# Third batch's softmax and second weights' split placed behind the second batch's last first-step evictions, on one Trainium2 core

## The chip, the cores and the metric

One of the cores of a Trainium2 chip runs the whole program. The metric is the device time of one execution in microseconds (us). Five engines work side by side, each through its own queue of instructions and in that queue's order: PE (matrix products), DVE (VectorE), ACT (ScalarE), POOL (GpSimd) and SP, which here only starts DMAs. An instruction at the head of a queue waits until what it needs is there, and all behind it wait with it.

## The reference

For each of 8 batches, x is 4224 rows of 192 columns. Each row has 8 heads of 24 columns, and each head has 7 weights.

```python
w = weight_gen - np.max(weight_gen, axis=-1, keepdims=True)
w = np.exp(w)
w = w / (np.sum(w, axis=-1, keepdims=True) + 1e-09)       # softmax over the 7 taps
...
out = np.einsum('bshk,bskhg->bshg', w, x_unf)              # causal convolution, 7 rows, weights by row and head
...
X = np.fft.fft(x, axis=1)                                  # x is now the convolution's result
X = np.fft.fft(X, axis=2)
mixed = np.real(X).astype(np.float32)
u = x + mixed
un = (u - mu) / np.sqrt(var + 1e-06)                       # over the 192 columns
ch = np.maximum(un @ w_ch1, 0.0) @ w_ch2                   # 192 -> 768 -> 192
return (u + ch).astype(np.float32)
```

The two weights of the last line come as 64-bit floats.

## The kernel before

A batch's 4224 rows lie as 33 slots of 128 partitions. Five stages follow each other in a batch, and stages of neighbouring batches overlap. In names below, b is the batch, c a chunk and g a group.

*Softmax* (`softmax_taps`). DVE takes the maximum over the taps (L279) and subtracts it (L280), ACT takes Exp in place (L282), DVE sums (L284), adds 1e-9 (L285) and takes the reciprocal (L286) into a PSUM tile `wp`. From batch 2 on this is done for all 33 slots at once (`parts` of one piece). The generator yields between the steps, and `tap_step(b, n)` drives it to its n-th yield: the first follows the load of the weights, the second the Exp, the third the reciprocal.

*Convolution* (`conv`). Chunks 0 to 7 hold four slots each, chunk 8 (`NC`) a single one. Per chunk DVE makes the normalized weights `wp` (L372 and L375), then seven products (L441): the first straight into `u`, the others into `pr`, from a ring of five buffers. POOL adds each `pr` to `u` (L450). `DVE_ADDS` names the chunks of which DVE makes the first adds: in batch 1's chunks 2 to 7 the first two. POOL then folds mirrored slots into `sm` (L464, L466), PE takes the first step of the Fourier transform into `pg` (L471), ACT copies parts of it into `gt` and `up` (L476, L478), DVE adds and subtracts (L480, L482) into `gt`, and `gt` goes to DRAM as `g_d` (L485, L486), two chunks at a time.

*Transform* (`transform`). `g` is read back from `g_d` in another layout (L507), PE takes the second step into `pp` (L517), and ACT copies it into `pq` (L521 to L531). All of `g_d` must be there first, chunk 8 too.

*Mix and norm* (`mix`, `norm`). PE takes the transform over the columns into `eo` (L546), ACT copies half of it to `ot` (L551), DVE adds to `u` (L552 to L561). ACT takes the row statistics (L586, L590, L592), POOL a product (`rs`, L599), ACT normalizes into `un` (L601) and rounds to 16 bits into `hl` (L609), POOL writes the rest of the rounding into `hl` (L610, L612), and a transposing DMA makes `ht` (L618).

*MLP* (`mlp`). Group n is four slots, n = 9b + g. PE makes the first layer in six pieces `ph` of five terms (L643), ACT the relu `hh` (L653, or L649 in the first groups), DVE the rest of its rounding (L654). In the same stretch PE makes the second layer `po` of group n - 1 (L666), DVE adds it to `u` (L671), and `u` goes out (L675). The first seven groups (`F32_GROUPS`) use the second weights in 32 bits (`w2f`); later ones use two 16-bit parts, `w2h` and `w2l`. `split_w2` makes these: three maxima on DVE (L179), a trip through PE to have the largest of all partitions (L186, L189), a scale, then per third an ACT product into `w2h` (L220) and a DVE product less that into `w2l` (L221), and a factor `isc`.

*What sets the order.* Each stage is a stream of pieces with a start and an end, in units of MLP groups, and `run` takes the stream that is furthest behind. Then a planner simulates the queues and sets the order in which instructions really stand in them. `tc.issue_after(ins)` holds what is issued under it in that plan until after `ins`; `queue(ins, ...)` and `behind(ins, gen)` are built on it. The streams around the change:

```python
add(SPLIT + 1.0, SPLIT + 1.5, late_split())
...
pp_at, mix_at, step = (NG - HELD + 0.6, NG - HELD, 0.6) if b == 1 else (PP_AT, 3.0, MIX_STEP)
```

`late_split` is issued behind group 4's `ph` and behind batch 1's last product. The transform of batch 1 begins at 9 - 2.6 = 6.4, and from 7.0 on `held_mlp` holds group 7 until batch 1's last `pp` is issued. Batch b's convolution is issued behind the last product of batch b - 1 (`next_conv`).

Of the kernel before, what the change touches and what calls it, by code (L numbers as in the profile page):

```python
# [31 lines left out]
EARLY = 7.4  # L32
HELD = 7.0
SPLIT = 4
CONV_LEAD = 0.4
# [3 lines left out]
POOL_TAPS = {(0, 0): (5, 6), (0, 1): (5, 6), (0, 3): (6,), (1, 0): range(7), (1, 1): range(7)}  # L39
DVE_ADDS = {(1, c): 2 for c in range(2, NC)}  # L40
F32_GROUPS = 7
# [51 lines left out]
def tile_dynconv_fnet_mlp(  # L93
# [159 lines left out]
    def prep_w2(i):  # L253
        words_to_f32(loaded[1][i], w2_part(i)[0], f"w2_{i}", ("po", 2))

    def split_w2(_):
        s2 = weight_scale([w2_part(i)[0].bitcast(I32) for i in range(NH // 2)], 32, "w2")
        for i in range(NH // 2):
            split_f32(*w2_part(i), s2)
        nc.vector.tensor_tensor(out=isc, in0=scales[0][:, 1:2], in1=s2[:, 1:2], op=ALU.mult)  # L260
# [3 lines left out]
    def softmax_taps(b, parts):  # L264
# [5 lines left out]
        for lo, hi in parts:  # L270
# [3 lines left out]
            elif b == 0 and hi < N2:  # L274
# [6 lines left out]
                                    in1=m[:, sl].unsqueeze(2).broadcast_to([P, n, K]), op=ALU.subtract)  # L281
            nc.scalar.activation(w_sb[:, sl], w_sb[:, sl], AF.Exp)  # L282
            yield None
# [4 lines left out]

    taps = {}

    def tap_step(b, n):
# [15 lines left out]
    def conv(b):  # L307
# [22 lines left out]
        def need_taps(c):  # L330
            nonlocal w_sb, ws
            while not rows_w.issuperset(rows_of(c)):
                i = next(part_iter)
                rows_w.update(range(*parts[i]))
                tap_step(b, 3 * i + 3)
                w_sb, ws = taps[b]["tiles"]
# [14 lines left out]
        for grp in groups:  # L351
# [101 lines left out]
            while tails and not (b == 1 and grp[0] == 0):  # L453
# [23 lines left out]
                up = sb.tile([P, 2, D - DH], F32, tag="up", name=f"up_{b}_{c}", bufs=2)  # L477
                nc.scalar.copy(up[:, 0:J], pg[:, 0:J, DH:D])  # L478
                fwd, rev = pg[:, 0:J, 1:DH - 1], up[:, 0:J, ::-1]
# [53 lines left out]
    state, us, hls = {}, {}, {}  # L533
    last_tile, last_pg, last_product, last_fold, last_gt, last_g2, last_pp = {}, {}, {}, {}, {}, {}, {}
    pending = {}
# [207 lines left out]
    def late_split():  # L743
        yield 0.0
        with tc.issue_after(last_ph[SPLIT].ins):
            queue(last_product[1].ins, (split_w2, None))
        yield 1.0
# [20 lines left out]
    add(0.93, 0.95, late_warm(1))  # L768
    add(SPLIT + 1.0, SPLIT + 1.5, late_split())
    for b in range(B):  # L770
        t0 = NG * b
        pp_at, mix_at, step = (NG - HELD + 0.6, NG - HELD, 0.6) if b == 1 else (PP_AT, 3.0, MIX_STEP)
        if b > 0:
# [46 lines left out]
```

## Time and profile before

| | us |
|---|---|
| median of 3 runs | 1138.15 |
| lowest, highest | 1135.78, 1138.86 |
| span of the profiled execution | 1136.8 |
| PE busy in it | 1082.2 |
| DVE busy | 968.2 |
| POOL busy | 866.7 |
| ACT busy | 814.5 |

The span is from the first to the last instruction of one execution, which a hardware profiler recorded; all rows of the trace come from it, and its times count from the span's start. The profile gives no other time of that execution, so its span stands for its own time; it lies within the range of the three runs. A row of the timeline has the start, the length, the engine, the line, the operation, output and inputs, the shape, how many such instructions in a row were put together (x3), and in brackets how long the engine was idle just before and what it waited for. Lengths include a start-up that overlaps the instruction before, so from start to start is often less than a length. Matrix products in 32 bits count double in the x. A row of the windows has the length of the stretch, the busy time of PE, PE's weight loads, DVE, ACT and POOL, then the granted clock of PE as a share of full speed, the share of the DMA engines and GB/s.

The single slot of batch 1 is added up in POOL's row at 207.41, the last `gt` of batch 1 is written at 215.29, the Exp of batch 2 runs at 206.68, and PE takes batch 1's first `pp` at 223.50.

### The profile page before, as it was taken

How to read it: one execution, taken by the hardware profiler on the slowest of the kernel's cores; microseconds unless marked ns; L12 is line 12 of the kernel's file. 1: busy time of each engine (PE TensorE's matmuls, PEld its weight loads, DVE VectorE, ACT ScalarE, POOL GpSimd, SP SyncE). 2: the span in 40 equal slices, each digit the busy share in tenths (PEclk: the TensorE clock that was granted, in tenths of full speed). 3: DMA queues.
4: the chain of work that ended last, by engine and by line, in shares of the span. 5: the costliest groups of instructions: out<-in, count | busy, mean ns of one | idle time of the engine just before them, and what ended most of it. 6: DMA issues, size and time to landing. Idle time of an engine off the chain costs nothing.

```text
span 1136.8 us, 23769 instructions
## 1 busy us (share of the span) xinstructions
PE 1082.2 (95%) x8476; PEld 819.3 (72%) x8476; DVE 968.2 (85%) x1797; ACT 814.5 (72%) x2556; POOL 866.7 (76%) x747
## 2 busy tenths in 40 slices
PE   5986999999999999899999999999999999999998
PEld 3454677787777767677767877777768877787777
DVE  7988999879989999899988999999989996356443
ACT  4666785468975798568974799568965898589822
POOL 5979588699979999599969999699959999012200
PEclk9996999999999999999999999999999999999999
DMA  8353244614473248414562348414661234413221
GB/s 304 129 150 106 56 110 123 175 51 128 111 200 92 65 119 219 122 55 119 149 165 81 94 107 218 121 44 119 170 140 50 71 74 98 115 43 74 70 47 46
DMA packets 156504, 128.74 MB, mean 113 GB/s; under 512 B 108571, under 2 KB 133088, under 8 KB 156384
## 3 DMA queue, kind: packets, MB, share of 16 engines
q1 hardware_dynamic: 156384, 127.21, 42.2%
q8 instruction: 67, 1.10, 0.4%
q14 instruction: 53, 0.43, 0.1%
HBM read 61.46 MB, written 39.37 MB: 89 GB/s over the span
## 4 chain that ended last, share of the span: by engine, by line
PE 52%; DVE 16%; ACT 11%; issue 8%; POOL 7%; DMA 6%; SPq 1%; DVEq 0%; POOLq 0%; ACTq 0%
PE ph L643 22%; PE po L666 19%; DVE pr L441 6%; POOL u L450 6%; PE pp L517 4%; PE eo L546 3%; DMA g<-g_d 2%; ACT junk L590 2%; ACT junk L586 2%; PE pg L471 2%; PE pa L446 2%; ACT hh L653 2%; ACT un L601 2%; DVE hh L654 2%; DMA g_d<-gt 1%
## 5 line engine op out<-in xcount | busy, mean ns | idle before, releaser
L450 POOL TENSOR_TENSOR u<-u,pr 128x768 f32<-128x768 f32 (+1 forms) x390 | 644.5, 1675 | 71.0 <-DVE pr L441 49.6
L666 PEld LDWEIGHTS <-hh 128*128 128x128 f16 x4248 | 364.0, 98 | 74.1 <-DVE hh L654 2.2
L666 PE MATMUL po<-w2h,hh 128*128 128x192 f16 x2832 | 413.9, 246 | 1.2 <-DVE hh L654 1.0
L643 PE MATMUL ph<-ht,w1h 128*128 128x512 f16 (+1 forms) x1296 | 397.0, 363 | 5.4 <-DMA ht<-hl 2.5
L441 DVE TENSOR_TENSOR pr<-x_sb,wp 128x768 f32<-128x768 f32 (+1 forms) x415 | 354.5, 877 | 13.7 <-POOL u L450 9.9
L666 PE MATMUL po<-w2l,hh 128*128 128x192 f16 x1416 | 345.2, 246 | 0.0
L654 DVE SCALAR_TENSOR_TENSOR hh<-ph,hh 128x512 f16<-128x512 f32 (+1 forms) x390 | 246.4, 637 | 108.0 <-ACT hh L653 107.4
L653 ACT ACTIVATE hh<-ph 128x512 f16<-128x512 f32 (+1 forms) x390 | 213.3, 550 | 140.8 <-PE ph L643 114.6
L643 PE MATMUL ph<-ht,w1l 128*128 128x512 f16 (+1 forms) x864 | 311.2, 363 | 0.0
L643 PEld LDWEIGHTS <-w1h 128*128 128x128 f16 x1296 | 126.1, 99 | 93.2 <-issue 2.3
L601 ACT ACTIVATE un<-u,rs 128x192 f32<-128x192 f32 x264 | 123.7, 536 | 16.7 <-POOL hl L612 5.5
L643 PEld LDWEIGHTS <-w1l 128*128 128x128 f16 x864 | 85.4, 99 | 52.9 <-issue 5.3
L590 ACT ACTIVATE junk<-u,rs 128x192 f16<-128x192 f32 x252 | 114.2, 454 | 3.6
L610 POOL TENSOR_TENSOR hl<-un,hl 128x512 f16<-128x512 f32 (+1 forms) x69 | 75.2, 1090 | 51.9 <-issue 26.5
L586 ACT ACTIVATE junk<-u 128x192 f16<-128x192 f32 x252 | 90.8, 360 | 21.5 <-DVE u L556 17.9
L521 ACT COPY pq<-pp 97x204 f32<-97x204 f32 (+1 forms) x96 | 46.9, 489 | 57.4 <-PE pp L517 57.0
L546 PE MATMUL eo<-cs_sb,pq 97*128 97x97 f32 x544 | 84.2, 277 | 2.7 <-DVE u L556 2.7
L546 PEld LDWEIGHTS eo<-cs_sb,pq 97*128 97x128 f32 x544 | 78.1, 195 | 10.2 <-issue 4.7
L671 DVE SCALAR_TENSOR_TENSOR u<-po,isc,u 128x384 f32<-128x384 f32 (+1 forms) x122 | 72.8, 597 | 9.1 <-PE po L666 9.0
L464 POOL TENSOR_TENSOR sm<-u 128x382 f32<-128x382 f32 x64 | 65.3, 1021 | 5.8 <-DMA g_d<-gt 2.8
L599 POOL TENSOR_TENSOR rs<-rs 128x4 f32<-128x4 f32 (+1 forms) x63 | 12.8, 206 | 70.7 <-DVE rs L593 70.6
L666 PE MATMUL po<-w2f,hh 128*128 128x192 f32 x336 | 62.6, 328 | 0.0
(110 smaller groups left out, 1319.5 us busy)
## 6 DMA issues: line engine op xcount, KB each, us to landing
out_dram<-u SPq DMA_DIRECT2D x64, 384.0 KB
x_sb<-in_x_dram SPq DMA_DIRECT2D x48, 384.0 KB
g<-g_d SPq DMA_DIRECT2D x40, 336.0 KB
x_sb<-in_x_dram SPq DMA_DIRECT2D x8, 864.0 KB
g_d<-gt SPq DMA_DIRECT2D x32, 195.0 KB
g_d<-gt SPq DMA_DIRECT2D x32, 189.0 KB
w<-in_weight_gen_dram SPq DMA_DIRECT2D x6, 924.0 KB
x_sb<-in_x_dram SPq DMA_DIRECT2D x8, 672.0 KB
```

Source lines behind the costliest of these rows:

```text
L441: last_product[b] = nc.vector.tensor_tensor(out=dst, in0=rows, in1=wk, op=ALU.mult)
L450: adder.tensor_tensor(out=u, in0=u, in1=pr, op=ALU.add)
L546: nc.tensor.matmul(eo[:, e, j, :], lhsT=pq[0:DH, e, r, r:r + P], rhs=cs_sb[:, e, :], start=True, stop=True)
L586: nc.scalar.activation(junk, uv[:, t, :], AF.Identity, accum_out=st[:, t, 0:1])
L590: nc.scalar.activation(junk, uv[:, t, :], AF.Square, bias=rs[:, 2, t:t + 1], accum_out=st[:, t, 1:2])
L601: nc.scalar.activation(halves[t // 2][:, t % 2, :], uv[:, t, :], AF.Identity, bias=rs[:, 1, t:t + 1], scale=rs[:, 0, t:t + 1])
L610: lo_eng.tensor_tensor(out=hl[:, t0:t1, 2 * P:3 * P], in0=src[:, 0:t1 - t0, 0:P], in1=hl[:, t0:t1, 0:P], op=ALU.subtract)
L643: last_ph[n] = nc.tensor.matmul(ph[:, 0:T], lhsT=wt[:, cs_], rhs=ht[:, 0:T, blk], start=(i == 0), stop=(i == len(terms) - 1))
L653: nc.scalar.activation(a[:, 0:T], ph[:, 0:T], AF.Relu)
L654: nc.vector.scalar_tensor_tensor(out=l[:, 0:T], in0=ph[:, 0:T], scalar=0.0, in1=a[:, 0:T], op0=ALU.max, op1=ALU.subtract)
L666: nc.tensor.matmul(po[t // 2][:, t % 2, :], lhsT=hx[:, t], rhs=wx[:, c2, :], start=(c2 == 0 and i == 0), stop=(c2 == NH - 1 and i == len(t ...
L671: nc.vector.scalar_tensor_tensor(out=lt, in0=po[t // 2][:, 0:t % 2 + 1], scalar=scales[0][:, 1:2] if f32 else isc, in1=lt, op0=ALU.mult, o ...
```

## The change

- The softmax of batch 2 (the third): Exp is issued behind batch 1's last `up` copy, which is that of chunk 8, and sum, 1e-9 and reciprocal behind batch 1's last `gt`. Maximum and subtraction are issued as before. `tap_step` is called in two steps for that in every batch.
- `split_w2` is divided: `scale_w2` takes the scale (maxima, the trip through PE), behind batch 1's last product as before; the products into `w2h` and `w2l` and `isc` are issued behind batch 1's last `gt`. The stream `late_split` moves from 5.0 to 5.5 to 6.4 to 6.5.
- `DVE_ADDS` gets `(1, NC): KW`: the six adds of batch 1's single slot (128x192) are on DVE and not on POOL.
- `PP_1` names the 2.6 of batch 1's transform, whose value is as before.

```diff
-DVE_ADDS = {(1, c): 2 for c in range(2, NC)}
+PP_1 = 2.6
+DVE_ADDS = {**{(1, c): 2 for c in range(2, NC)}, (1, NC): KW}
...
+    def scale_w2(_):
+        scales.append(weight_scale([w2_part(i)[0].bitcast(I32) for i in range(NH // 2)], 32, "w2"))
+
     def split_w2(_):
-        s2 = weight_scale([w2_part(i)[0].bitcast(I32) for i in range(NH // 2)], 32, "w2")
+        s2 = scales[1]
         for i in range(NH // 2):
             split_f32(*w2_part(i), s2)
...
-            nc.scalar.activation(w_sb[:, sl], w_sb[:, sl], AF.Exp)
+            with after(last_up[1].ins if b == 2 else None):
+                nc.scalar.activation(w_sb[:, sl], w_sb[:, sl], AF.Exp)
...
+    def after(ins):
+        return tc.issue_after(ins) if ins is not None else nullcontext()
...
-                tap_step(b, 3 * i + 3)
+                tap_step(b, 3 * i + 2)
+                with after(last_gt[1].ins if b == 2 else None):
+                    tap_step(b, 3 * i + 3)
...
-                nc.scalar.copy(up[:, 0:J], pg[:, 0:J, DH:D])
+                last_up[b] = nc.scalar.copy(up[:, 0:J], pg[:, 0:J, DH:D])
...
         with tc.issue_after(last_ph[SPLIT].ins):
-            queue(last_product[1].ins, (split_w2, None))
+            queue(last_product[1].ins, (scale_w2, None))
+            queue(last_gt[1].ins, (split_w2, None))
...
-    add(SPLIT + 1.0, SPLIT + 1.5, late_split())
+    add(NG - PP_1, NG - PP_1 + 0.1, late_split())
...
-        pp_at, mix_at, step = (NG - HELD + 0.6, NG - HELD, 0.6) if b == 1 else (PP_AT, 3.0, MIX_STEP)
+        pp_at, mix_at, step = (PP_1, NG - HELD, 0.6) if b == 1 else (PP_AT, 3.0, MIX_STEP)
```

Lines of the changed kernel have higher numbers: by 1 up to the weights' helpers, by 4 or 5 in `softmax_taps`, by 10 from there on.

The planner makes more of it than the diff tells, so here is what stands in three queues. A name such as `gt_1_8_2093` is the tile, batch, chunk and a running number.

ACT at the end of batch 1's convolution, before:

```order
L478 COPY up_1_6_1945<-pg_1_6_1940 128x190
L282 ACT_TABLE_LOAD
L282 ACTIVATE w_2_2110<-w_2_2110 128x1848
L220 ACTIVATE w2h_85<-w2f_87,sc_w2_1855 128x384 x3
L649 ACTIVATE hh_0_5_3_1962<-ph_0_5_3_1950 128x512
L649 ACTIVATE hh_0_5_4_1984<-ph_0_5_4_1975 128x512
L649 ACTIVATE hh_0_5_5_2002<-ph_0_5_5_1993 128x512
L476 COPY gt_1_6_1943<-pg_1_7_2043 128x4
L478 COPY up_1_7_2047<-pg_1_7_2043 128x190
L476 COPY gt_1_8_2093<-pg_1_8_2091 128x2
L478 COPY up_1_8_2095<-pg_1_8_2091 128x95
L649 ACTIVATE hh_0_6_0_2035<-ph_0_6_0_2015 128x512
```

And in the changed kernel:

```order
L659 ACTIVATE hh_0_6_0_2010<-ph_0_6_0_1990 128x512
L486 COPY gt_1_6_1918<-pg_1_7_2018 128x4
L488 COPY up_1_7_2022<-pg_1_7_2018 128x190
L659 ACTIVATE hh_0_6_1_2035<-ph_0_6_1_2029 128x512
L486 COPY gt_1_8_2068<-pg_1_8_2066 128x2
L488 COPY up_1_8_2070<-pg_1_8_2066 128x95
L287 ACT_TABLE_LOAD
L287 ACTIVATE w_2_2110<-w_2_2110 128x1848
L659 ACTIVATE hh_0_6_2_2078<-ph_0_6_2_2059 128x512
L221 ACTIVATE w2h_85<-w2f_87,sc_w2_2095 128x384 x3
```

Exp and the split have moved from ahead of the copies of `pg` to behind them, and between those of chunk 7 and chunk 8 there is now a relu of group 6. On PE `pg_1_8` stood directly behind `pg_1_7`; now five `po` of group 5 and eight `ph` of group 6 stand between them, the trip of the scale through PE follows behind, and the first `pp` has as much of group 6 ahead of it as before.

DVE at the same place, before:

```order
L284 TENSOR_REDUCE wp_2_2109<-w_2_2110 128x264
L221 SCALAR_TENSOR_TENSOR w2l_86<-w2f_87,sc_w2_1855,w2h_85 128x384 x3
L285 TENSOR_SCALAR wp_2_2109<-wp_2_2109 128x264
L671 SCALAR_TENSOR_TENSOR u_0_4_337<-po_0_4_1_1837,sc_w1_889,u_0_4_337 128x384
L286 RECIPROCAL wp_2_2109<-wp_2_2109 128x264
L480 TENSOR_TENSOR gt_1_6_1943<-pg_1_7_2043,up_1_7_2047 128x2x95
L482 TENSOR_TENSOR gt_1_6_1943<-pg_1_7_2043,up_1_7_2047 128x2x95
L480 TENSOR_TENSOR gt_1_8_2093<-pg_1_8_2091,up_1_8_2095 128x95
L482 TENSOR_TENSOR gt_1_8_2093<-pg_1_8_2091,up_1_8_2095 128x95
L372 TENSOR_TENSOR wp_2_2109<-w_2_2110,wp_2_2109 128x224
L441 TENSOR_TENSOR u_2_0_2121<-x_sb_66,wp_2_2109 128x768
L441 TENSOR_TENSOR pr_2_0_1_2124<-x_sb_66,wp_2_2109 128x768
```

And now (between the rows on scales, of one column each, nothing else is left out than a `po` eviction):

```order
L492 TENSOR_TENSOR gt_1_8_2068<-pg_1_8_2066,up_1_8_2070 128x95
...
L289 TENSOR_REDUCE wp_2_2109<-w_2_2110 128x264
L191 TENSOR_SCALAR m2_w2_2088<-me_w2_2092 128x1
L290 TENSOR_SCALAR wp_2_2109<-wp_2_2109 128x264
...
L291 RECIPROCAL wp_2_2109<-wp_2_2109 128x264
L264 TENSOR_TENSOR isc_88<-sc_w1_889,sc_w2_2095 128x1
L222 SCALAR_TENSOR_TENSOR w2l_86<-w2f_87,sc_w2_2095,w2h_85 128x384 x3
L382 TENSOR_TENSOR wp_2_2109<-w_2_2110,wp_2_2109 128x224
L681 SCALAR_TENSOR_TENSOR u_0_5_466<-po_0_5_1_1989,sc_w1_889,u_0_5_466 128x384
L451 TENSOR_TENSOR u_2_0_2121<-x_sb_66,wp_2_2109 128x768
L451 TENSOR_TENSOR pr_2_0_1_2124<-x_sb_66,wp_2_2109 128x768
```

The sum, the reciprocal and the split stood ahead of the last `gt`; all of them now stand behind it, and ahead of batch 2's first products.

DVE at the end of batch 2's convolution, before:

```order
L286 RECIPROCAL wp_3_3710<-wp_3_3710 128x264
L654 SCALAR_TENSOR_TENSOR hh_1_5_1_3731<-ph_1_5_1_3702,hh_1_5_1_3731 128x512
L480 TENSOR_TENSOR gt_2_8_3619<-pg_2_8_3617,up_2_8_3621 128x95
L482 TENSOR_TENSOR gt_2_8_3619<-pg_2_8_3617,up_2_8_3621 128x95
L372 TENSOR_TENSOR wp_3_3710<-w_3_3711,wp_3_3710 128x224
L441 TENSOR_TENSOR u_3_0_3722<-x_sb_66,wp_3_3710 128x768
```

And now:

```order
L492 TENSOR_TENSOR gt_2_8_3619<-pg_2_8_3617,up_2_8_3621 128x95
L664 SCALAR_TENSOR_TENSOR hh_1_6_1_4002<-ph_1_6_1_3996,hh_1_6_1_4002 128x512
L290 TENSOR_SCALAR wp_3_3710<-wp_3_3710 128x264
L664 SCALAR_TENSOR_TENSOR hh_1_6_2_4041<-ph_1_6_2_4032,hh_1_6_2_4041 128x512
L681 SCALAR_TENSOR_TENSOR u_1_5_1737<-po_1_5_0_3944,isc_88,u_1_5_1737 128x384
L291 RECIPROCAL wp_3_3710<-wp_3_3710 128x264
L664 SCALAR_TENSOR_TENSOR hh_1_6_3_4072<-ph_1_6_3_4057,hh_1_6_3_4072 128x512
L382 TENSOR_TENSOR wp_3_3710<-w_3_3711,wp_3_3710 128x224
L451 TENSOR_TENSOR u_3_0_3722<-x_sb_66,wp_3_3710 128x768
```

Batch 2's last `gt` now stands some way further on in the MLP (group 15, whose tiles are `hh_1_6`, is at work there, and before it was group 14), and the reciprocal of batch 3 stands behind it. In POOL's queue the rounding rests `hl` of batch 1 stand six or seven adds of batch 2 earlier than before, and that of batch 2's first group two adds of batch 3 earlier. On PE the sum of the work is the same, and so is the work ahead of group 18's first `ph`; batch 2's `pg`, `pp` and `eo` stand further back among it.

More of the change, by code (lines that the diff above doesn't have):

```diff
@@ L1 @@
-from contextlib import ExitStack
+from contextlib import ExitStack, nullcontext
 import numpy as np
@@ L533, in tile_dynconv_fnet_mlp @@
     state, us, hls = {}, {}, {}
-    last_tile, last_pg, last_product, last_fold, last_gt, last_g2, last_pp = {}, {}, {}, {}, {}, {}, {}
+    last_tile, last_pg, last_product, last_fold, last_gt, last_up, last_g2, last_pp = {}, {}, {}, {}, {}, {}, {}, {}
     pending = {}
```

## The prediction

> **What bounds the kernel now.** I read the page first (which engine is full), then the time by windows (where the full engine is not), then the waits and the chain of waits there, and at last the timeline of each engine at those places.
>
> ```profile
> PE 1082.2 (95%) x8476; PEld 819.3 (72%) x8476; DVE 968.2 (85%) x1797; ACT 814.5 (72%) x2556; POOL 866.7 (76%) x747
> ...
> 217.78:334.00 116.22, 111.61 (x868) 86.99 (x867) 103.11 (x186) 90.49 (x287) 113.14 (x95) 0.99 0.46 120
> 220.00:240.00 20.00, 16.50 (x119) 13.92 (x117) 13.73 (x18) 10.99 (x30) 19.84 (x13) 0.91 0.44 113
> 223.50:227.60 4.10, 4.09 (x22) 4.05 (x23) 3.45 (x5) 2.32 (x7) 4.10 (x3) 0.58 0.44 88
> 380.00:400.00 20.00, 17.84 (x180) 15.24 (x179) 19.68 (x43) 17.89 (x68) 19.91 (x18) 0.94 0.39 99
> 400.00:420.00 20.00, 20.00 (x145) 13.84 (x144) 17.75 (x32) 19.36 (x72) 18.90 (x17) 0.97 0.44 111
> ```
>
> PE is the bound of the whole, with 95%. The windows (length, then busy time of PE, its weight loads, DVE, ACT, POOL, and the granted clock) show two of the places where it is not full: 220 to 240 us, batch 1's transform, and 380 to 400 us, the first group of batch 2. Between them, while batch 2 is convolved, POOL works 113.14 of 116.22 us: it is the bound of that stretch, and what it finishes late comes late to PE.
>
> ```profile
> 209.95 0.81 PE L471 MATMUL pg<-sm,f_sb 128*128 128x192 f32 x4
> 210.60 0.49 PE L471 MATMUL pg<-u,f_sb 128*128 128x192 f32 x2
> ...
> 223.50 1.57 PE L517 MATMUL pp<-te_sb,g 102*97 102x102 f32 x8 [2.48 <-DMA g<-g_d]
> 227.61 0.38 PE L643 MATMUL ph<-ht,w1h 128*128 128x512 f16 x1
> 230.21 0.87 PE L517 MATMUL pp<-te_sb,g 102*97 102x102 f32 x8
> 230.91 0.86 PE L517 MATMUL pp<-to_sb,g 102*97 102x102 f32 x8
> ```
> ```profile
> 208.46 2.09 DVE L284 TENSOR_REDUCE wp<-w 128x264 f32<-128x1848 f32 x1 [0.99 <-ACT w L282]
> 210.45 1.67 DVE L221 SCALAR_TENSOR_TENSOR w2l<-w2f,sc_w,w2h 128x384 f16<-128x384 f32 x3
> 212.03 0.44 DVE L285 TENSOR_SCALAR wp<-wp 128x264 f32<-128x264 f32 x1
> 212.38 0.61 DVE L671 SCALAR_TENSOR_TENSOR u<-po,sc_w,u 128x384 f32<-128x384 f32 x1
> 212.90 1.81 DVE L286 RECIPROCAL wp<-wp 128x264 f32<-128x264 f32 x1
> 214.62 0.34 DVE L480 TENSOR_TENSOR gt<-pg,up 128x190 f32<-128x190 f32 x1
> 215.29 0.25 DVE L482 TENSOR_TENSOR gt<-pg,up 128x95 f32<-128x95 f32 x1
> 215.46 0.39 DVE L372 TENSOR_TENSOR wp<-w,wp 128x224 f32<-128x224 f32 x1
> 215.88 0.95 DVE L441 TENSOR_TENSOR u<-x_sb,wp 128x768 f32<-128x768 f32 x1
> 216.75 5.27 DVE L441 TENSOR_TENSOR pr<-x_sb,wp 128x768 f32<-128x768 f32 x6
> ...
> 217.78 16.40 POOL L450 TENSOR_TENSOR u<-u,pr 128x768 f32<-128x768 f32 x9 [8.42 <-DVE pr L441]
> ```
>
> The first step of batch 1's last two chunks (pg) is done at about 211, but its evictions (gt, from 214.62) stand on DVE behind batch 2's sum, the split of the weights and the reciprocal. The last ends at 215.54; the trip through DRAM then takes until 223.50, PE waits 2.48 us, and in the 4.10 us after it its clock is 0.58. The same queue shows the other side: the softmax is what POOL waits for, 8.42 us, and its first add of batch 2 is at 217.78.
>
> **The change, part by part.** *A, PE at batch 1's transform.* In the new order the softmax and the split stand behind the last gt, but pg of the single row is moved too: five ph and five po stand between it and pg of chunk 7. By the spacing of rows (ph 0.216, po f32 0.326) that is 1.08 + 1.63, with three ph more 3.4 us. So it is at 210.60 + 3.4 = 214.0; its copies end 1.26 later as now (row below), at 215.2, and the two adds of 0.25 make 215.7. The last gt is no earlier (215.54 now). PE, however, has 2.3 us more work ahead of pp, comes at 223.3 where g lands near 223.7, and the 2.48 is all but gone. The halved clock goes with it: from 223.50 to 227.61 run sixteen pp and six po, 4.11 us; at the spacing of 230.21 to 230.91 (0.70 for eight) and of 0.163 they take 1.40 + 0.98 = 2.38, so 1.73 more. A is -2.48 - 1.73 = -4.2 (ends -2.5, the clock falls anyway, and -4.2).
>
> The Trainium skill, "TensorE: Matmul & The Clock Gate", sections Part 1 and Why this matters for your kernels, lets the clock fall after a window of about 3.4 us without work and calls gaps up to about 3 us harmless; by that a 2.48 us wait has no such price and A would be -2.5. The trace shows 0.58 behind it, and decides; no run shows what the gate counts.
>
> *B, batch 2's first add on POOL.* Exp now is issued behind the last up copy.
>
> ```profile
> 211.58 0.28 ACT L478 COPY up<-pg 128x95 f32<-128x95 f32 x1
> ...
> 204.97 1.28 ACT L282 ACT_TABLE_LOAD   x1
> 206.68 1.75 ACT L282 ACTIVATE w<-w 128x1848 f32<-128x1848 f32 x1 [0.43 <-DVE w L280]
> ```
>
> 215.2 + 1.28 (table) + 1.75 = 218.2. Behind it on DVE, by starts of rows above: sum 2.0 = 220.2; +1e-9, 0.35, and three scale operations of one column, some 0.3 = 220.9; reciprocal 1.72 = 222.6; isc 0.2; w2l 1.58 = 224.4; wp 0.42; one po eviction 0.52 = 225.3; u 0.87, the first pr 0.87 = 227.0; the add starts 0.16 later. **227.2 instead of 217.78: +9.4.** Nothing hides it: POOL has no other work there, and its idle time grows from 8.42 to about 18. The six single-row adds taken from POOL (0.65 each) therefore bring nothing, and on VectorE (about 0.3 each) they stand ahead of the place where it waits for Exp. The w2l and isc are used only by later po, and cost only these 1.8 us in the queue. Max and subtract stay where they are.
>
> *C, to the end of batch 2's convolution.*
>
> ```profile
> 263.63 1.16 POOL L610 TENSOR_TENSOR hl<-un,hl 128x512 f16<-128x512 f32 x1 [2.42 <-ACT hl L609]
> 332.73 1.26 POOL L450 TENSOR_TENSOR u<-u,pr 128x192 f32<-128x192 f32 x2
> 335.67 0.43 POOL L610 TENSOR_TENSOR hl<-un,hl 128x128 f16<-128x128 f32 x1 [1.68 <-ACT hl L609]
> ...
> 336.86 0.52 PE L471 MATMUL pg<-u,f_sb 128*128 128x192 f32 x2
> 340.71 0.25 DVE L482 TENSOR_TENSOR gt<-pg,up 128x95 f32<-128x95 f32 x1
> 343.19 9.41 POOL L450 TENSOR_TENSOR u<-u,pr 128x768 f32<-128x768 f32 x5 [6.83 <-DVE pr L441]
> ```
>
> POOL's path: its last single-row add ends at 334.0 now. +9.4, plus 0.74 for the small hl that now stands ahead of it, gives 344.1 if the wait of 2.42 stays, 341.7 if it goes. I let it stay, since hl of group 10 now stands seven adds earlier in POOL's queue. pg followed that add by 2.9; if it follows at once it comes at 344.3 or 341.9. PE's path: counted by the spacings above, (po f16 0.082, pp 0.088, eo 0.22 besides) 277.5 us of matmuls stand ahead of this pg before and 288.6 now; 336.86 + 11.1 - 4.2 = 343.8. The later one: C = **+7.4** (ends 5.0, if PE too is quicker, and 10.1).
>
> *D, from there to batch 3's first add.* Now 343.19 - 336.86 = 6.33. In the new order wp of batch 3 stands behind the fourth hh of group 15, which needs its ph: 5.3 us of matmuls behind pg, then relu 0.6, hh 0.6, wp 0.42, u 0.87, pr 0.87 and hand-overs 0.2, together 8.9. D = +2.5 (ends 0, pg being later than its place, and +3).
>
> *E, to the first group of batch 2.*
>
> ```profile
> 368.85 0.61 PE L546 MATMUL eo<-cs_sb,pq 97*128 97x97 f32 x4
> 390.16 1.81 POOL u L450
> 393.81 3.68 DMA ht<-hl
> 397.53 5.08 PE ph L643 x15
> ...
> PE ph L643 <- DMA ht<-hl: 1.1, 1, 1.1
> ```
>
> PE's wait there ends with the transposing DMA of hl, which stands on POOL behind batch 3's adds: 25 of them before, 23 now, each 1.78. E = -3.6, and by POOL ph of group 18 is late by 7.4 + 2.5 - 3.6 = +6.3.
>
> A second path to the same ph goes by PE alone. Batch 2's first eo has 308.6 us of matmuls ahead of it, ph of group 18 has 334.6, 26.0 between; the trace has 397.53 - 368.85 = 28.7, the length of the chain through the mix, the norm and the transpose, and PE idles for the rest. Now eo has 320.2 ahead and ph still 334.6: only 14.4 of work to fill the chain. If it takes 28.7 again, ph comes 11.6 - 4.2 = +7.4 later. There is less other work on ACT and DVE inside it; taking out that which the new queues no longer have there leaves about 27, so +5.7. Both paths agree; I take **+7** (ends +2, if the chain shrinks by 5, and +12).
>
> **Sum:** A's 4.2 us are waited away at group 18, and what is left is the +7. The clock behind this wait is halved already (0.94 and 0.97 in the windows), so a longer wait costs 0 more (up to 1.7). The rest of the program has the same matmuls; the later batches are only reshuffled, and I take nothing for them (-2 to +2). The profiled execution lasted 1136.8 us, 1.3 under the median of 1138.15; 1136.8 + 7 = 1143.8 for a like run, 1145 by the median. Ends: +2 - 2 = 0 and 12 + 1.7 + 2 = +16.
>
> **Rivals.**
> *PE alone counts, faster.* If group 18's ht lands by the time PE comes (397.53 - 1.14 - 4.2 = 392.2), the 4.2 us remain: 1134. For it: PE's 95%, and POOL idles 6.83 us at the end of batch 2 and more at the next, so lateness could be caught there:
>
> ```profile
> 469.74 3.70 POOL L450 TENSOR_TENSOR u<-u,pr 128x768 f32<-128x768 f32 x2 [8.24 <-DVE pr L441]
> ```
>
> Against it: these waits are for products that themselves wait for gt, and the chain of waits at 397.53 goes through POOL's adds without slack. It wins if batch 2's first add is late by less than about 1 us, or if POOL can make up all of it. Chance 0.17. The Trainium skill, "Perfetto Trace Analysis", section Identifying the Most-Contended Engine, says to improve the engine of highest occupancy first; by that rule this rival is the forecast, but it also says that regimes differ, and in this one POOL's 113.14 of 116.22 is the highest.
>
> *No change.* B comes out at about 5 instead of 9.4 (Exp and sum overlap better than their queues say) or half of the lateness is absorbed: +3 at group 18, less what the reshuffled rest may give; 1135 to 1141.6. Chance 0.15.
>
> *Worse.* C at its upper end and DVE's hh, queued behind products that wait for POOL's buffers, hold po as well: 10.1 + 3 - 3.6, the clock 1.7 and the rest 2 make +13, 1151 and above. Chance 0.08.
>
> *The forecast*, 1141.6 to 1151: 0.60.
>
> **How the numbers follow.** A measurement can tell 0.3% (3.4 us) here: faster is below 1134.7, slower above 1141.6. Faster 0.17, same 0.15, slower 0.60 + 0.08 = 0.68. The range 1135.5 to 1152.5 leaves out some 0.13 below and 0.05 above.
>
> **What would show it.** A: no wait at batch 1's first pp, clock near 1 in the 4 us behind it. B: Exp at 216 to 217, batch 2's first POOL add near 227. C and D: pg of batch 2's single row near 344, batch 3's first add near 352. E: ph of group 18 near 404.5, with a wait of PE ahead of it of over 10 us. If that ph starts before 400, the forecast is wrong and the first rival right.

## The result and the profile after

The change makes the kernel slower: median 1155.13 us (1153.0 to 1158.04, 4 runs) against 1138.16 (1135.78 to 1138.86, 4 runs), ratio 1.0161 [1.0142, 1.018], or 17 us. Forecast were 1145 and 1152.5 at the most: the sign was right, the size not. The profiled execution of the changed kernel took 1154.15 us, with a span of 1152.4, so a run lasts 1.75 us longer than its span. By that, the run behind the profile before would have taken about 1138.6, and not 1.3 us under the median, as the prediction has it.

From the page and from two answers by windows, the changed kernel first, then the kernel before:

```profile
PE 1083.6 (94%) x8476; PEld 820.4 (71%) x8476; DVE 974.0 (85%) x1803; ACT 822.3 (71%) x2556; POOL 864.6 (75%) x741
...
220.69:224.80 4.11, 4.11 (x39) 3.44 (x38) 4.11 (x7) 3.28 (x10) 0.60 (x1) 1.00 0.42 123
380.00:400.00 20.00, 12.26 (x113) 11.59 (x111) 18.45 (x39) 17.33 (x66) 20.00 (x17) 0.79 0.18 55
400.00:420.00 20.00, 17.40 (x100) 11.01 (x101) 17.75 (x34) 18.87 (x65) 20.00 (x19) 0.79 0.61 130
...
340.00:405.00 65.00, 52.45 (x471) 44.31 (x470) 59.41 (x102) 43.25 (x133) 50.61 (x37) 0.90 0.29 80
```
```profile
340.00:405.00 65.00, 62.19 (x550) 48.95 (x548) 63.60 (x114) 43.17 (x138) 61.17 (x44) 0.97 0.33 95
```

PE has the same work (1083.6 and 1082.2 us). In the 65 us around batch 2's first group it idles 12.55 us, before 2.81. The four microseconds behind batch 1's first `pp`, which had a clock of 0.58, now run at 1.00.

The timeline of PE, and then of DVE, ACT and POOL, of the changed kernel:

```profile
220.69 0.86 PE L527 MATMUL pp<-te_sb,g 102*97 102x102 f32 x8
...
342.46 0.49 PE L481 MATMUL pg<-u,f_sb 128*128 128x192 f32 x2
...
376.46 0.61 PE L556 MATMUL eo<-cs_sb,pq 97*128 97x97 f32 x4
...
389.05 1.10 PE L556 MATMUL eo<-cs_sb,pq 97*128 97x97 f32 x8 [1.20 <-DVE u L566]
395.48 1.65 PE L481 MATMUL pg<-sm,f_sb 128*128 128x192 f32 x4 [5.33 <-POOL sm L476]
...
400.11 1.99 PE L556 MATMUL eo<-cs_sb,pq 97*128 97x97 f32 x8 [1.33 <-DVE gt L492]
404.59 0.58 PE L653 MATMUL ph<-ht,w1h 128*128 128x512 f16 x1 [2.48 <-DMA ht<-hl]
```
```profile
212.69 0.25 DVE L492 TENSOR_TENSOR gt<-pg,up 128x95 f32<-128x95 f32 x1
...
213.79 1.75 ACT L287 ACTIVATE w<-w 128x1848 f32<-128x1848 f32 x1
...
218.17 1.82 DVE L291 RECIPROCAL wp<-wp 128x264 f32<-128x264 f32 x1
...
223.17 5.27 DVE L451 TENSOR_TENSOR pr<-x_sb,wp 128x768 f32<-128x768 f32 x6
...
224.20 16.41 POOL L460 TENSOR_TENSOR u<-u,pr 128x768 f32<-128x768 f32 x9 [22.10 <-DVE pr L451]
...
337.81 1.26 POOL L460 TENSOR_TENSOR u<-u,pr 128x192 f32<-128x192 f32 x2
...
353.99 14.76 POOL L460 TENSOR_TENSOR u<-u,pr 128x768 f32<-128x768 f32 x8 [14.92 <-DVE pr L451]
```

The last `gt` of batch 1 is written at 212.94 (before 215.54) and `pp` has no wait. The price is where it was forecast: the first add of batch 2 stands at 224.20 instead of 217.78 and POOL has waited 22.10 us. The first `ph` of group 18 starts at 404.59; the prediction said 404.5. Ahead of it PE waits four times in one chain (1.20, 5.33, 1.33, 2.48), which makes the 10 us that it had named.

That agreement is in part luck. Up to about 150 us both kernels hold the same instructions in the same order, yet this execution is 3.69 us ahead by the first `ph` of group 1 (124.87 against 128.57). Other runs stand there between -2.70 and +1.61. Below, lateness is the start of a group's first `ph` less that of the profiled execution before, and "own" is the same less its value at group 1. The changed kernel at group 18 is +7.06, own +10.75; at its end +15.53, own +19.2. So some 8.5 us more are lost behind group 18, where the prediction took nothing.

The waits of PE from 410 to 1130 us, before and then of the changed kernel (columns: total, times, longest):

```profile
PE pp L517 <- DMA g<-g_d: 7.8, 5, 2.9
PE ph L643 <- DMA ht<-hl: 1.4, 2, 1.0
PE eo L546 <- DVE u L556: 0.4, 1, 0.4
PE ph L643 <- DVE hh L654: 0.3, 1, 0.3
```
```profile
PE pp L527 <- DMA g<-g_d: 7.2, 5, 2.7
PE ph L653 <- DMA ht<-hl: 5.6, 3, 3.5
PE po L676 <- DVE hh L664: 2.1, 4, 0.7
PE ph L653 <- DVE hh L664: 0.4, 1, 0.4
```

9.9 us before and 15.5 after (with one row of 0.2 that is not shown): later batches too wait longer for the first `ht` of a batch.

### The profile page after: what moved, and what is told of

It is laid out like the page before. It is cut to its first block, busy times and chain, and to the rows that moved or that the text cites. A ratio compares the mean times of both kernels' runs of the same rounds, so it can differ in the third digit from the quotient of the medians.

```text
span 1152.4 us, 23765 instructions
## 1 busy us (share of the span) xinstructions
PE 1083.6 (94%) x8476; PEld 820.4 (71%) x8476; DVE 974.0 (85%) x1803; ACT 822.3 (71%) x2556; POOL 864.6 (75%) x741
## 4 chain that ended last, share of the span: by engine, by line
PE 63%; DVE 13%; ACT 9%; DMA 7%; issue 4%; POOL 3%; SPq 1%; DVEq 0%; ACTq 0%; POOLq 0%
PE ph L653 27%; PE po L676 23%; PE pp L527 5%; DVE pr L451 5%; PE eo L556 3%; DMA g<-g_d 2%; PE pg L481 2%; POOL u L460 2%; DMA g_d<-gt 2%; ACT pr L419 2%; ACT junk L596 1%; ACT junk L600 1%; DVE hh L664 1%; DMA ht<-hl 1%; DVE u L460 1%
## 5 line engine op out<-in xcount | busy, mean ns | idle before, releaser
L653 PEld LDWEIGHTS <-w1l 128*128 128x128 f16 x864 | 85.3, 99 | 62.1 <-issue 13.9
L681 DVE SCALAR_TENSOR_TENSOR u<-po,isc,u 128x384 f32<-128x384 f32 (+1 forms) x122 | 73.3, 601 | 11.6 <-PE po L676 11.6
```

Of the source, the lines that this page charges most:

```text
L653: last_ph[n] = nc.tensor.matmul(ph[:, 0:T], lhsT=wt[:, cs_], rhs=ht[:, 0:T, blk], start=(i == 0), stop=(i == len(terms) - 1))
L681: nc.vector.scalar_tensor_tensor(out=lt, in0=po[t // 2][:, 0:t % 2 + 1], scalar=scales[0][:, 1:2] if f32 else isc, in1=lt, op0=ALU.mult, o ...
```

## The experiments

Two theories stood against each other; the expectations call them theory 1 and theory 3. *Lateness*: batch 2's convolution starts late because the softmax does, and POOL cannot catch up. *Order*: the edit makes the planner write another order into every queue, for all later batches too, and since the queues are worked through in that order, the order itself costs the time, whether or not the softmax is late. Theory 2 of the expectations, that the split ahead of batch 2's products makes them late, is a part of the first. All ratios are against the kernel before, run on the same chip. The lateness of every run by group is in a table at the end of this section.

### One part of the change at a time

*The softmax alone*: from the changed kernel, the split and the six adds as before.

```diff
-DVE_ADDS = {**{(1, c): 2 for c in range(2, NC)}, (1, NC): KW}
+DVE_ADDS = {(1, c): 2 for c in range(2, NC)}
...
-            queue(last_product[1].ins, (scale_w2, None))
-            queue(last_gt[1].ins, (split_w2, None))
+            queue(last_product[1].ins, (scale_w2, None), (split_w2, None))
...
-    add(NG - PP_1, NG - PP_1 + 0.1, late_split())
+    add(SPLIT + 1.0, SPLIT + 1.5, late_split())
```

> Only the softmax of batch 2 is moved behind batch 1's last evictions; the second weights' split and the single-row adds stay as in the kernel before. Theory 1 (the late softmax makes POOL's convolution of batch 2 late, and that reaches group 18): first POOL add of batch 2 at 222 to 225 us against 217.8, ph of group 18 at 403 to 406 with PE waiting over 9 us ahead of it, total 1147 to 1156. Theory 2 (the split and the trip of its scale, standing ahead of batch 2's first products on VectorE, make it late): without them the first add is back at 219 to 220, the total at 1140 to 1144. Theory 3 (every new plan of the queues loses time at the later batches, whatever is moved): ph of group 18 as late as by theory 1 or less, and 4 to 8 us more lost between groups 18 and 54.

Measured: 1149.92, ratio 1.0129 [1.0082, 1.0176], at group 18 own +10.2, at group 54 own +16.9, which fits theories 1 and 3 alike. The softmax alone, with the order that the planner then writes, brings the whole loss up to group 18; this run can't tell which of the two makes it.

*The split alone*: from the changed kernel, Exp and reciprocal without `after`, `DVE_ADDS` as before.

```diff
-            with after(last_up[1].ins if b == 2 else None):
-                nc.scalar.activation(w_sb[:, sl], w_sb[:, sl], AF.Exp)
+            nc.scalar.activation(w_sb[:, sl], w_sb[:, sl], AF.Exp)
...
-                tap_step(b, 3 * i + 2)
-                with after(last_gt[1].ins if b == 2 else None):
-                    tap_step(b, 3 * i + 3)
+                tap_step(b, 3 * i + 3)
```

> Only the second weights' split is moved (scale, then products behind batch 1's last evictions); softmax and single-row adds stay as before. Theory 1: no loss, since the softmax is in time: the last gt of batch 1 is about 1.6 us earlier (the three low halves no longer stand ahead of it), first add of batch 2 at 217 to 219, total 1133 to 1139. Theory 2: first add at 220 or later, total 1142 to 1147. Theory 3: 4 to 8 us lost behind group 18: 1141 to 1146.

Measured: 1156.5, ratio 1.0174 [1.0147, 1.02], as much as the whole change and above what any theory expected, though no softmax is late. 16 us of it come between groups 45 and 54, 600 us behind the edit. The waits of PE from 840 to 862 us and a window behind them:

```profile
PE pp L524 <- DMA g<-g_d: 8.7, 1, 8.7
...
849.40:859.60 10.20, 5.60 (x27) 4.43 (x28) 4.91 (x7) 2.35 (x6) 10.04 (x7) 0.50 0.51 136
```

At batch 6's transform the new order lets PE wait 8.7 us for `g`, and for 10.2 us, from inside that wait on, the clock is at half. Nothing of the split works there any more; the run with the split in the old order, below, shows that it is the order.

*The six adds alone*: softmax and split as before, `DVE_ADDS` as changed.

> Only the six single-row adds of batch 1 go to VectorE. Theories 1 and 2: nothing to be measured, 1135 to 1141, first add of batch 2 within 1 us of 217.8. Theory 3: a new plan here too, so 4 to 8 us lost behind group 18: 1141 to 1146.

Measured: 1146.2, ratio 1.0086 [1.0057, 1.0114]; the time is near what theory 3 expected, the place is not. It is own +9.3 by group 9 already: `pg` of the single row is issued at 219.65 (before 210.60), and PE then waits at batch 1's first `pp`:

```profile
233.57 1.65 PE L524 MATMUL pp<-te_sb,g 102*97 102x102 f32 x8 [4.35 <-DVE pr L448]
```

*All but the softmax*: split and adds together.

> The changed kernel with only the softmax of batch 2 back at its old place (split and single-row adds as changed). Theory 1: the loss is gone, 1132 to 1140; no wait of over 3 us ahead of group 18's ph. Theory 2: the loss stays by half or more, 1145 to 1152. Theory 3: 1141 to 1146, lost behind group 18.

Measured: 1140.59, ratio 1.004 [1.0024, 1.0056]. Split alone +20 us and adds alone +10 us make +4 together. Costs of parts that each get an order of their own do not add; a part's cost can't be read from such a kernel.

### The parts in the old order

To part lateness from order, the next kernels hold every queue to a written order: `pin(tc)`, called once all is issued, ties each instruction to the one ahead of it in a table of the queues, and the planner no longer decides. The table is that of the kernel before, with only the named instructions put elsewhere; the diffs show rows of these queues.

*Only an output DMA moved*, on SP, the one that writes group 5's rows.

```diff
-L675 DMA out_dram<-u_5_466 128x768
 L507 DMA g_1_16_2237<-g_d_90 112x4x192
 L507 DMA g_1_20_2264<-g_d_90 112x192
 L509 DMA g_1_20_2264<-g_d_90 68x192
+L675 DMA out_dram<-u_5_466 128x768
```

> The kernel before in its old order, only the output of group 5 moved behind the transform's readings of g in SP's queue. Splits the run with the reciprocal behind into its two parts: 1135 to 1138 if that queue cost little before (0 to 1.5 us of pacing at 230 to 240 us), 1132 to 1134 if it is most of what that run gains.

Measured: 1137.72, ratio 1.0011 [0.9993, 1.0029]; own lateness within 0.3 up to group 18. So holding the order, with this one move, costs nothing that can be measured.

*The split behind the last `gt`*, all else in the old order; on ACT the products into `w2h` go behind the second relu of group 6. DVE's queue:

```diff
-L260 TENSOR_TENSOR isc<-sc_w_889,sc_w_1855 128x1
 L284 TENSOR_REDUCE wp_2109<-w_2110 128x264
-L221 SCALAR_TENSOR_TENSOR w2l<-w2f,sc_w_1855,w2h 128x384 x3
...
 L482 TENSOR_TENSOR gt_8_2093<-pg_8_2091,up_8_2095 128x95
+L260 TENSOR_TENSOR isc<-sc_w_889,sc_w_1855 128x1
+L221 SCALAR_TENSOR_TENSOR w2l<-w2f,sc_w_1855,w2h 128x384 x3
```

> The kernel before in its old order, only that the products of the second weights' split stand behind batch 1's last evictions; the softmax stays. If the 20 us of the run with the split alone were the plan's: 1131 to 1138, last gt of batch 1 some 1.6 us earlier, no wait of over 4 us at batch 6's first pp. If the split itself costs them: over 1145.

Measured: 1137.85, ratio 1.0003 [0.9983, 1.0023]. The split's place costs nothing that can be measured (2.6 us at the most, by the interval); the 20 us of the split alone were its order.

*The six adds of the single row on DVE*, all else in the old order:

```diff
-DVE_ADDS = {(1, c): 2 for c in range(2, NC)}
+DVE_ADDS = {**{(1, c): 2 for c in range(2, NC)}, (1, NC): KW}
...
+    pin(tc)
```

> Old order in every queue, only the six single-row adds of batch 1 on VectorE, each behind its product. If the 10 us of the run with these adds alone were the new plan's: 1135 to 1140. If the adds themselves cost them: over 1143.

Measured: 1140.16, ratio 1.004 [1.0024, 1.0057]. PE waits 2.5 us for the scale's trip, which now stands behind these adds on DVE, and 2.5 at `pp`, as the kernel before does too. So the adds themselves cost 3.4 us by the medians (2.7 to 6.5 by the interval); the other 6 of the kernel with adds alone came by its order.

*A alone*: Exp and sum stay, the reciprocal goes behind the last `gt`, the split behind the first chunk's products, and the output DMA behind `g` as above. DVE's queue:

```diff
-L286 RECIPROCAL wp_2109<-wp_2109 128x264
...
 L482 TENSOR_TENSOR gt_8_2093<-pg_8_2091,up_8_2095 128x95
+L286 RECIPROCAL wp_2109<-wp_2109 128x264
...
 L671 SCALAR_TENSOR_TENSOR u_5_466<-po_5_0_2013,sc_w_889,u_5_466 128x384
+L260 TENSOR_TENSOR isc<-sc_w_889,sc_w_1855 128x1
+L221 SCALAR_TENSOR_TENSOR w2l<-w2f,sc_w_1855,w2h 128x384 x3
```

> Old order in every queue, with these moves by hand: only the reciprocal of batch 2 stands behind batch 1's last gt (Exp, sum and 1e-9 stay ahead of it), the split's products stand behind the products of batch 2's first chunk, and the output of group 5 behind the transform's readings of g. If the theory of the late softmax is right, this takes the gain at the transform without its price: last gt at 212 to 213 against 215.5, first POOL add of batch 2 at 216 to 217.5, ph of group 18 early by 1 to 4 us, total 1131 to 1136, 1 to 5 under the kernel before. If the transform's wait was no loss at all: 1136 to 1139.

Measured: 1137.02, ratio 0.9991 [0.9972, 1.0011]. Windows of this kernel and of the kernel before, and the two longest waits of PE from 210 to 300 us of this kernel:

```profile
220.00:240.00 20.00, 19.00 (x145) 15.70 (x144) 16.91 (x21) 11.63 (x32) 16.66 (x11) 1.00 0.41 110
240.00:300.00 60.00, 56.17 (x433) 43.16 (x433) 56.94 (x109) 47.48 (x165) 59.92 (x49) 0.97 0.29 80
```
```profile
240.00:300.00 60.00, 58.89 (x466) 46.51 (x464) 57.05 (x110) 48.95 (x174) 57.25 (x47) 1.00 0.30 81
```
```profile
PE ph L643 <- DVE hh L654: 1.4, 1, 1.4
PE ph L643 <- DMA ht<-hl: 1.1, 1, 1.1
```

The wait and the half clock at the transform are gone: PE is busy 19.00 of 20 us instead of 16.50, and by group 7 the run is own -4.2, just what A was sized at. In the next 60 us PE is busy 2.72 less, and at group 9 the gain is down to -0.5: POOL is full there (59.92 of 60), and PE only comes earlier to waits for `hh` and `ht`, with a clock of 0.97 over these 60 us. At group 18 own +0.5 is left.

*Softmax and split in the old order*, each at the place that the change names; the six adds stay on POOL. DVE and ACT:

```diff
-L284 TENSOR_REDUCE wp_2109<-w_2110 128x264
-L221 SCALAR_TENSOR_TENSOR w2l<-w2f,sc_w_1855,w2h 128x384 x3
-L285 TENSOR_SCALAR wp_2109<-wp_2109 128x264
-L286 RECIPROCAL wp_2109<-wp_2109 128x264
...
 L482 TENSOR_TENSOR gt_8_2093<-pg_8_2091,up_8_2095 128x95
+L284 TENSOR_REDUCE wp_2109<-w_2110 128x264
+L285 TENSOR_SCALAR wp_2109<-wp_2109 128x264
+L286 RECIPROCAL wp_2109<-wp_2109 128x264
+L221 SCALAR_TENSOR_TENSOR w2l<-w2f,sc_w_1855,w2h 128x384 x3
...
-L282 ACTIVATE w_2110<-w_2110 128x1848
...
 L478 COPY up_8_2095<-pg_8_2091 128x95
+L282 ACTIVATE w_2110<-w_2110 128x1848
```

> The kernel before with every queue held to its old order, only that Exp, sum, 1e-9 and reciprocal of batch 2 and the products of the split are put behind batch 1's last evictions by hand, in the order that the changed kernel has there (the single-row adds stay on POOL). This is the change without a new plan. Theory 1 (late softmax): last gt of batch 1 at 212.5 to 213.5, PE's wait at the first pp gone, batch 2's first POOL add at 222 to 224 against 217.8, ph of group 18 late by 3 to 6 us, total 1139 to 1144. If all of the loss is the plan's: ph of group 18 early by 2 to 4 us, total 1131 to 1136.

Measured: 1141.8, ratio 1.0061 [1.0035, 1.0087]. A wait in the middle of batch 1's transform, and the window behind it:

```profile
239.71 1.65 PE L517 MATMUL pp<-te_sb,g 102*97 102x102 f32 x8 [6.60 <-DMA g<-g_d]
...
236.10:249.80 13.70, 9.76 (x39) 7.82 (x40) 7.01 (x9) 2.98 (x9) 13.70 (x10) 0.50 0.22 64
```

This is a cost of SP, which the prediction did not look at. On SP the output of group 5 stands ahead of the next reading of `g`. It waits for an eviction on DVE that now stands behind batch 2's first products, so it is issued at 235.26 (before 230.84), and `g` behind it at 235.72 (before 231.81), by the trace's issues on SP. The lateness of +8 arises there and stays.

*The same with that output DMA behind the readings of `g`*, by the first diff of this part.

> As the change in the old order, and in SP's queue the output of group 5 is put behind the transform's last reading of g, so that those readings no longer wait for an eviction that stands behind batch 2's products on VectorE. If the 6.8 us wait inside batch 1's transform was that queue: it is gone, PE is 3 to 5 us ahead at groups 7 to 9. What is left is the late softmax alone: by theory 1 (POOL's lateness is the loss) batch 2's first POOL add is still 5 to 7 us late and ph of group 18 4 to 7 us, with a longer wait of PE ahead of it, total 1139 to 1144. If only the queue was the loss and POOL can catch up: ph of group 18 early, total 1131 to 1135.

Measured: 1140.34, ratio 1.0024 [1.0007, 1.0042]; own +3.6 at group 18. The first add of batch 2 stands at 221.0, 5.1 us late by own start, and POOL's last single-row add only 2.4: POOL makes up 2.7. So softmax and split at these places cost 3 us (0.8 to 4.8 by the interval), and with the adds' 3.4 it is some 6 of the 17. That is an estimate: all three together in the old order were not run, and the first add is later in the changed kernel (own +10.1).

### Old and new order by stretches

Four kernels take their table in pieces from the queues of the two kernels, and change from one to the other at the first `ph` of a group. The first and third are the changed kernel's program, the second and fourth that of the kernel before; the diff of each is `pin(tc)` alone.

*New order until group 7, then the old one.* The softmax is late as in the changed kernel.

> The changed kernel with its own order up to group 7's first ph (just ahead of batch 2's first POOL add), the old order behind it. The first add is late as in the changed kernel (9 to 10 us, counted from the run's own start). If that lateness alone makes the 10.7 us at group 18: ph of group 18 is 9 to 12 us late here too, total 1146 to 1150. If the new order between there and group 18 makes about half: the old order lets POOL catch up 2 to 4 us, ph of group 18 is 4 to 7 us late, total 1140 to 1145.

Measured: 1144.11, ratio 1.0067 [1.0046, 1.0088]; own +8.0 at group 18 and no more to the end.

```profile
225.81 3.74 POOL L460 TENSOR_TENSOR u<-u,pr 128x768 f32<-128x768 f32 x2 [22.09 <-DVE pr L451]
...
243.38 1.65 PE L481 MATMUL pg<-sm,f_sb 128*128 128x192 f32 x4 [5.45 <-POOL sm L476]
```

In the old order PE comes to batch 2's first `pg` early and waits 5.45 us there for the late adds. The +8.0 lies between the two forecasts: the old order lets POOL make up a part of the 10 us, and the late add still costs most of them.

*Old order until group 7, new order to group 18, then the old one.* The softmax is in time.

> The counterpart: old order up to group 7's first ph, the changed kernel's order from there to group 18's first ph, old order behind it. Batch 2's first add is in time. If lateness alone counts: ph of group 18 within 2 us of the kernel before, total 1135 to 1139. If the new order in between costs by itself (batch 2's eo stand only 14.5 us of matmuls ahead of group 18's ph, so that PE idles there): ph of group 18 is 4 to 9 us late, total 1141 to 1147.

Measured: 1153.78, ratio 1.0151 [1.0135, 1.0167]; own +12.3 at group 18. POOL and DVE of this kernel, then PE and the window:

```profile
215.21 16.41 POOL L450 TENSOR_TENSOR u<-u,pr 128x768 f32<-128x768 f32 x9 [8.42 <-DVE pr L441]
...
236.29 0.69 DVE L654 SCALAR_TENSOR_TENSOR hh<-ph,hh 128x512 f16<-128x512 f32 x1 [9.92 <-ACT hh L653]
...
244.87 5.37 POOL L450 TENSOR_TENSOR u<-u,pr 128x768 f32<-128x768 f32 x3 [10.35 <-DVE pr L441]
...
340.30 1.26 POOL L450 TENSOR_TENSOR u<-u,pr 128x192 f32<-128x192 f32 x2
...
407.14 0.59 PE L643 MATMUL ph<-ht,w1h 128*128 128x512 f16 x1 [2.67 <-DMA ht<-hl]
...
340.00:405.00 65.00, 54.53 (x488) 45.84 (x487) 59.60 (x100) 41.93 (x128) 49.62 (x38) 0.91 0.27 79
```

The first add is at 215.21, in time by own start (+0.1), and yet the loss up to group 18 is there, and more of it than either theory expected. DVE stands 9.92 us at the first `hh` of group 7 with batch 2's products behind it, so POOL runs dry for 10.35 us. PE idles 10.47 of the 65 us around group 18. A late first add is not needed for the loss.

But the run does not take POOL's lateness away: its last single-row add of batch 2 ends at 341.56, own +10.3 (in the changed kernel at 339.07, own +8.8). The lateness comes from another place, at which the changed kernel itself hardly waits, because there the products are late already:

```profile
233.97 0.69 DVE L664 SCALAR_TENSOR_TENSOR hh<-ph,hh 128x512 f16<-128x512 f32 x1 [1.23 <-ACT hh L663]
```

So in the new order a softmax in time brings nothing. Whether POOL's lateness or the order of PE's work makes the loss at group 18 this run can't tell, since both are in it.

*New order until group 18, then the old one.*

> The changed kernel, each engine's queue held to the order it has in its own profile up to the first ph of group 18, and behind that to the order of the kernel before. Nothing else is changed. If the loss behind group 18 is made by the new order of the later batches: ph of group 18 is 7 us late as in the changed kernel, the lateness stays within 5 to 9 us to the end, total 1142 to 1147. If the loss is POOL's lateness that grows from batch to batch, whatever the order: over 14 us late at the end, total 1150 to 1156.

Measured: 1152.24, ratio 1.0144 [1.0125, 1.0163]. Lateness is +9.8 at group 18, +13.9 at group 27, and from there to the end it does not move (+13.8), whereas the changed kernel goes on from +11.4 at group 27 to +15.5. The ratio's interval overlaps that of the change, so a saving of some 3 us is likely but not shown by the times. By its time the run falls where the theory of lateness that grows whatever the order had it (1150 to 1156). The 4.0 us up to group 27 are some 0.4 under a clock still halved as group 18 begins, 1.9 at group 19's first `ph`, where PE waits 1.72 us for `ht`, and 1.7 behind a wait of 2.95 us at batch 3's first `pp`, where the clock is 0.91 over 20 us.

*Old order until group 18, then the new one.*

> The mirror: the kernel before in its own order up to the first ph of group 18, behind that in the changed kernel's order. If the order of the later batches makes the loss: 5 to 9 us are lost behind group 18 though nothing was late at it, total 1142 to 1147. If it is lateness that grows: nothing is late, so 1134 to 1140.

Measured: 1148.03, ratio 1.0097 [1.0067, 1.0126]. At group 18 it is in time (own 0.0), at group 27 own +5.7, at group 54 +12.3, at the end +10.3. Its longest waits of PE from 410 to 1130 us are those of the changed kernel:

```profile
PE pp L517 <- DMA g<-g_d: 5.9, 5, 1.7
PE ph L643 <- DMA ht<-hl: 5.7, 3, 3.6
PE po L666 <- DVE hh L654: 1.7, 4, 0.7
```

The later order costs 10 us with nothing late at its beginning, a little more than the 5 to 9 that were expected of it. Together with the run before: a late start at group 18 and the later order each cost something, and the two prices do not add.

Lateness of all runs in us at the first `ph` of a group, counted from the traces:

| kernel | group 1 | 9 | 18 | 27 | 54 | 71 | ratio |
|---|---|---|---|---|---|---|---|
| the change | -3.7 | -8.1 | 7.1 | 11.4 | 17.6 | 15.5 | 1.0161 |
| softmax alone | -2.0 | -4.4 | 8.2 | 8.2 | 14.9 | 18.9 | 1.0129 |
| split alone | 0.8 | 7.7 | 4.8 | 6.9 | 20.5 | 18.0 | 1.0174 |
| adds alone | 1.4 | 10.8 | 11.6 | 11.4 | 8.6 | 8.6 | 1.0086 |
| all but softmax | -1.2 | 4.1 | 3.8 | 0.2 | 2.5 | 0.0 | 1.004 |
| output DMA, old order | -1.6 | -1.9 | -1.8 | -1.8 | 0.1 | -0.1 | 1.0011 |
| split, old order | -1.0 | 1.3 | 1.5 | 3.0 | 1.4 | 1.5 | 1.0003 |
| adds, old order | -1.5 | 2.7 | 3.0 | 3.4 | 1.1 | 0.6 | 1.004 |
| A, old order | 1.2 | 0.7 | 1.7 | 4.5 | 2.2 | 1.6 | 0.9991 |
| softmax and split, old order | 1.6 | 8.0 | 8.1 | 9.2 | 8.7 | 8.8 | 1.0061 |
| the same, output DMA behind | -1.9 | 0.5 | 1.7 | 3.3 | 4.3 | 4.0 | 1.0024 |
| new until 7, old | -2.1 | 5.2 | 6.0 | 5.8 | 5.4 | 5.4 | 1.0067 |
| old, new 7 to 18, old | -2.7 | -5.7 | 9.6 | 15.4 | 13.5 | 13.2 | 1.0151 |
| new until 18, old | -2.0 | -6.3 | 9.8 | 13.9 | 13.9 | 13.8 | 1.0144 |
| old until 18, new | -2.1 | -3.8 | -2.1 | 3.6 | 10.2 | 8.2 | 1.0097 |

The softmax's row ends higher than its ratio because the profiled execution was the slowest of its four (1157.91). None of the kernels is faster than the one before.

## Why the prediction was wrong

**A, right in itself, wrongly credited.** The wait and the half clock went: with A alone PE was 4.2 us ahead behind them, and nothing of it was left at group 18. The changed kernel is own -4.4 at group 9 and own +11.3 at batch 2's first `eo` (376.46), where the sum by PE said 11.6 - 4.2. Windows from group 9's first `ph` to that `eo`, of the changed kernel and of the kernel before, and a wait of the changed kernel in between:

```profile
261.03:376.46 115.43, 111.07 (x909) 82.12 (x908) 105.77 (x181) 83.33 (x246) 99.44 (x86) 1.00 0.46 125
```
```profile
269.15:368.85 99.70, 98.68 (x802) 72.72 (x802) 94.69 (x163) 78.28 (x237) 90.56 (x79) 1.00 0.52 138
```
```profile
355.04 0.91 PE L527 MATMUL pp<-te_sb,g 102*97 102x102 f32 x8 [2.21 <-DMA g<-g_d]
```

The stretch is 15.7 us longer: 12.4 of it are matmuls (forecast 11.6), and 3.3 are waits, at which the sum put nothing. The longest is at batch 2's first `pp`, where PE waited 0.7 us before. Whether A was 2.5 or 4.2, by the rule or by the row, would have shifted the sum by 1.7 and not saved it.

**B, right.** +9.4 was forecast and +6.4 measured, or +10.1 by own start.

**C, D, E: the path by POOL.** `pg` of the single row came at 342.46 (forecast "near 344"), batch 3's first add at 353.99 ("near 352"), `ph` of group 18 at 404.59. By own start these are +9.3, +14.5 and +10.7, so that C was +9.3 (forecast +7.4), D +5.2 (+2.5) and E -3.8 (-3.6): two terms were too small, and the early start hid it. The path as such is real: with the old order behind group 7 the late add cost own +8.0 at group 18.

**The second path, by PE alone.** It fits the changed kernel: 111.07 of the 115.43 us are busy, and from that `eo` to `ph` of group 18 it takes 28.1 us (forecast 28.7, or about 27). The run with the new order in between takes the same 115.43 us for this stretch, though its softmax is in time. What the path lacked are the 3.3 us of waits. That it decides, and POOL does not, is not shown: POOL is late in both kernels.

**The step that failed**: "the later batches are only reshuffled, and I take nothing for them (-2 to +2)". The own lateness grows by 8.5 us behind group 18, 4.3 up to group 27 and 4.1 from there on. That the later order has a price is shown from a start in time: it alone costs own +10.3, ratio 1.0097. The reason given, that the matmuls are the same, is true (1083.6 against 1082.2 us busy) and says nothing on when PE may start them. How much of the 8.5 us the order makes in the changed kernel stays open: with the old order behind group 18 the 4 us up to group 27 are lost too, at other places, and only the growth behind it is gone. The smaller miss is the sum at group 18, own +10.7 for +7, by the waits named above.

**The rivals.** That PE alone counts is refuted by the run with A alone: 0.9991 for the very 4.2 us. The Trainium skill, "Perfetto Trace Analysis", section Identifying the Most-Contended Engine, has one begin with the engine of highest occupancy; here 4.2 us of wait and halved clock taken from the one with 95% moved nothing. For TensorE the section itself would judge by weight loads, here 72%, and not by matmul busy time, so that its rule does not plainly make this rival the forecast, as the prediction has it. "No change" came nearest for softmax and split in the old order (1.0024). "Worse", at 1151 and above, was what happened, but in part by another cause than it named.

Open stays why the planner's later order is worse on the chip than its earlier one. It was not tried to give the planner other durations, nor to move single instructions of the later batches. Open stays too how the 17 us divide between the late softmax and the order that was planned around it, since up to group 18 each of them alone loses most of what both lose together (own +8.0 and +12.3 against +10.7).

## What to carry to other kernels

Where a scheduler writes the queues, a local edit has two prices: its own, here an estimated 6 of 17 us, and that of the order that comes with it. Hold the order to measure the first, and before forecasting compare the whole new order with the old one, for each batch: how much work stands between the first product of a stage and its first use. A wait of the busiest engine is a loss only if nothing behind it would have made it wait anyway.

## What the runs showed of the chip

The half clock can last long. From inside the chain of waits at group 18 on, the changed kernel ran at half for 17 us in a row:

```profile
391.50:408.50 17.00, 9.21 (x30) 6.27 (x31) 14.95 (x30) 16.53 (x60) 17.00 (x17) 0.50 0.23 49
```

The length of a single wait does not tell whether the half clock comes. In the kernel before, the 2.48 us wait at batch 1's `pp` was followed by it, and the 2.92 us wait at batch 3's was not (its timeline and window):

```profile
473.82 0.94 PE L517 MATMUL pp<-te_sb,g 102*97 102x102 f32 x8 [2.92 <-DMA g<-g_d]
...
470.00:485.00 15.00, 12.07 (x111) 9.44 (x109) 13.15 (x19) 7.36 (x20) 13.36 (x8) 1.00 0.59 154
```

The Trainium skill, "TensorE: Matmul & The Clock Gate", section Why this matters for your kernels, puts the danger at gaps over about 3 us; the first of these waits lies below that and had it all the same.

An output DMA can hold an input. On SP a store that waits for its data kept the three readings behind it until 235.72; with the store behind them the same three were issued from 225.72 to 228.23 (the first is 6.5 us earlier by own start), and PE's wait of 6.60 us was gone.
